# Linformer attention and maxout FFN on one core: batch 2's softmax sums moved into one bank, their broadcast issued from GpSimd, and later turns of q

## The chip, the cores and the metric

The kernel runs on one core of one Trainium2 chip. The metric is the device time of one execution in microseconds. Four runs of the kernel before gave a median of 403.85 us (403.59 to 404.13). The execution that was profiled took 402.95 us; its span, from the first to the last instruction of the program, was 401.2 us. The clock that was granted to TensorE was 0.999 of full speed over it.

## What is computed

Two stages follow each other. The first is attention with projected keys and values, for 8 batches of 8 heads, 1024 positions and 64 features a head; the second is a feed-forward layer with three parallel weights.

```python
k_proj = np.einsum('ks,bhsd->bhkd', E, k)          # E, F: 64 x 1024
v_proj = np.einsum('ks,bhsd->bhkd', F, v)
scores = scale * np.matmul(q, k_proj.transpose(0, 1, 3, 2))
attn = np.exp(scores - max) ; attn = attn / (sum + 1e-9)
x = attn @ v_proj          # then (b, s) rows of 8 * 64 = 512
h = np.maximum(np.maximum(x @ w1, x @ w2), x @ w3)   # 512 -> 768
out = h @ w_out                                      # 768 -> 512, float32
```

The kernel leaves the maximum out of the softmax, works in bf16 on TensorE and adds in float32.

## The kernel before, in words

**Tiling.** A batch has 1024 rows, cut into two chunks of 512. For a chunk, `up` (L609) makes one of six blocks of 128 hidden features: 12 matmuls (3 weights by 4 slices of the 512 inputs) into three PSUM banks. ScalarE copies the first bank to SBUF (`h1s`, L625), VectorE takes the maximum with the second (`m12`, L629) and then with the third, which gives a block of `hT` (L577). `down` (L655) makes four tiles of 128 output rows, 6 matmuls each; from batch 1 on ScalarE copies each tile to SBUF, and after every second tile SyncE issues the store of both (L678). So a chunk has ten steps: 0 to 5 are `up`, 6 to 9 are `down`. PSUM has eight banks; attention takes pairs of banks (`two`) or single ones (`bank`).

**Attention is done one batch ahead.** While the feed-forward matmuls of batch b run, the attention of batch b + 1 is put between them. `plan(b)` (L685) says behind which step of which chunk each piece is issued: key (chunk, step). All queues (TensorE, VectorE, ScalarE, GpSimd, SyncE) run in program order, so this dictionary is the order of work. The pieces:

- `load(b)` (L197): three DMAs on GpSimd's queue, q, k and v of a batch, cast to bf16 (1 MB each in SBUF). q has two buffers, k and v one each. So k's load waits for the projection of the batch before, and v's as well. The load of q of batch b waits until the turn of q of batch b - 1 has landed.
- `qd(b)` (L380): VectorE copies q into `q_p` in four instructions, then SyncE issues one DMA transpose of `q_p` into `qT`.
- `kproj`, `vproj` (32 matmuls at L345, copies on VectorE and ScalarE) and `kt` (2 transposes at L412): the projected keys and values.
- `sc(b, g)`: scores of a pair of heads, 4 matmuls of 64 x 64 (L211) that run side by side; I call four such matmuls a pack. ScalarE then takes the exponential (`pT`, L222): at once with `now=True`, or else queued in `later`, which is run behind the next copy that ScalarE makes for `up` or `down`.
- `za(b, g)`, the older form of the softmax sums: a pack with `ones` as weights (the sums, spread over the partitions), a pack with the projected values, then on ScalarE `invert` (a logarithm at L291 and an exponential at L297, each over 128 x 1024) which writes `zi_all`, then on VectorE the product `xT` (`scale_x`, L308).
- `zc(b)` (L248), the newer form: 8 matmuls with `pick` (L256) put the sums of all heads into one bank; ScalarE takes one logarithm (L262) and one exponential (L265) of 128 x 512; SyncE stores the 32 KB result to DRAM (`zd`, L268) and then issues four DMAs (L275) that broadcast it to 64 partitions each of `zi_all`, 512 KB a DMA; the first two are for head pairs 0 and 1, the last two for 2 and 3. `vx(b, g)` follows later: the values pack and the product `xT`.

In the kernel before, batches 1 and 2 use `za` (batch 0 has its own start), batches 3 to 7 use `zc` and `vx`. Batch 1's pieces are issued during batch 0, batch 2's during batch 1, and so on.

Of the kernel before, what the change touches and what calls it, by code (L numbers as in the profile page):

```python
# [15 lines left out]
def kernel(  # L16
# [13 lines left out]
    nc = tc.nc  # L30
# [77 lines left out]
    def after(dma, earlier):  # L108
        tc.add_manual_dep(
            dma.ins, earlier.ins.name,  # L110
            mybir.DependencyInfo(
                mybir.DependencyClass.Sync, mybir.DependencyReason.DATA
            ),
        )


    def view(src, b):
        return src[b].rearrange("h (p si) d -> p h si d", si=SI)
# [12 lines left out]
    qkv, qTs, kpTs, vps, pTs, zis, xTs = {}, {}, {}, {}, {}, {}, {}  # L131
# [5 lines left out]
    def load_tiles(b):  # L137
        qkv[b] = tuple(
            loads.tile([P, H, SI, D], BF16, name=nm, bufs=n)
            for nm, n in (("q_t", 2), ("k_t", 1), ("v_t", 1))  # L140
        )
        return qkv[b]
# [51 lines left out]
    load_w(2, slice(2, 4))  # L194
    nc.gpsimd.dma_start(out=wout_sb, in_=moe_w_out.rearrange("(jt p) m -> p jt m", p=P))

    def load(b):  # L197
        tiles = load_tiles(b)
        for i in range(3):
            dma = nc.gpsimd.dma_start(out=tiles[i], in_=view((q, k, v)[i], b))  # L200
            if i == 0 and b - 1 in last_T:
                after(dma, last_T[b - 1])
# [42 lines left out]
            zi_alls[b] = att.tile([P, NPAIR, 2, CHUNK], FP32, name="zi_all", bufs=1)  # L245
        return zi_alls[b]

    def zc(b):  # L248

        def f():
            t, ns = bank()
            for hp in range(2):
                for g in range(NPAIR):
                    nc.tensor.matmul(  # L256
                        out=t[32 * g:32 * (g + 1), :], lhsT=pick[:, hp, :],
                        rhs=pTs[b, g, 0][:, hp, :], start=(hp == 0), stop=(hp == 1),
                    )
            ready = pe(2 * MM + 0.1)  # L260
            zlc = att.tile([P, CHUNK], FP32, name="zlc", bufs=1)
            nc.scalar.activation(out=zlc, in_=t, func=AF.Ln)  # L262
            runs("s", ready, 0.6, ns)
            zic = att.tile([P, CHUNK], FP32, name="zic", bufs=1)
            nc.scalar.activation(out=zic, in_=zlc, func=AF.Exp, scale=-1.0)  # L265
            when = runs("s", ready, 0.63) + 9.0
            zd = scratch.tile([NPAIR, 2, 2, CHUNK], FP32, name="zd")
            nc.sync.dma_start(  # L268
                out=zd.rearrange("g h c f -> (g h c) f"),
                in_=zic.rearrange("(a r) f -> a r f", r=8)[:, 0, :],  # L270
            )
            for u in range(2):
                gs = slice(2 * u, 2 * u + 2)
                for hp in range(2):
                    nc.sync.dma_start(  # L275
                        out=zi_all(b)[hp * HALF:(hp + 1) * HALF, gs],
                        in_=zd[gs, hp].partition_broadcast(HALF),
                    )
            for g in range(NPAIR):
                zis[b, g, 0] = zi_all(b)[:, g], when  # L280
        return f

    def vx(b, g):
        def f():
            scale_x(b, g, 0, SI, values(b, g, 0, SI))
        return f
# [34 lines left out]
    def sc(b, g, lo=0, nsi=SI, now=False):  # L321
        def f():
            t = scores(b, g, lo, nsi)
            if now:
                exps(b, g, lo, nsi, t)
            else:
                later.append(lambda: exps(b, g, lo, nsi, t))
        return f

    def za(b, g, lo=0, nsi=SI, then=False):  # L330
        def f():
            z = sums(b, g, lo, nsi)
            av = values(b, g, lo, nsi)
            invert(b, g, lo, nsi, z)
            if then:
                later.append(lambda: scale_x(b, g, lo, nsi, av))
            else:
                scale_x(b, g, lo, nsi, av)
        return f
# [40 lines left out]
    def qd(b, parts=1):  # L380

        def f():
            q_p = att.tile([P, NPAIR, SI, 2, D], BF16, name="q_p", bufs=1)
            qTs[b] = att.tile([P, NPAIR * SI, P], BF16, name="qT")
            n = NPAIR // parts
            for lo in range(0, NPAIR, n):
                for g in range(lo, lo + n):
                    copy(
                        "v", q_p[:, g].rearrange("p si h d -> p h si d"),
                        qkv[b][0][:, 2 * g:2 * g + 2], (), 0.43,  # L390
                    )
                last_T[b] = nc.sync.dma_start_transpose(
                    out=qTs[b][:, lo * SI:(lo + n) * SI, :],
                    in_=q_p[:, lo:lo + n].rearrange("p g si h d -> p (g si h d)"),
                )
        return f

    kps = {}
    def kproj(b):
        def f():  # L400
            t, ns = bank()
            proj(b, 1, t, (LO, HI), 4 * D)
            kps[b] = att.tile([P, 2, 2 * D], BF16, name="kp")
            copy("v", kps[b].rearrange("a g x -> a (g x)"), t[:, 0:4 * D], ns, 0.43)
        return f

    def kt(b):
        def f():
            t, ns = two()
            t = t.bitcast(BF16)[:, 0]  # L410
            for gg in range(2):
                nc.tensor.transpose(  # L412
                    out=t[:, gg * P:(gg + 1) * P], in_=kps[b][:, gg, :], identity=ident
                )
            pe(0.2)

            kpTs[b] = att.tile([P, NPAIR, KP], BF16, name="kpT")
            copy(
                "v", kpTs[b].rearrange("a (y x) k -> a x y k", x=2),
                t[:, 0:2 * P].rearrange("a (x y k) -> a x y k", x=2, y=2), ns, 0.3,  # L420
            )
        return f

    def vproj(b):
        def f():
            t, ns = bank()
            proj(b, 2, t, (LO, HI), 4 * D)

            vps[b] = att.tile([P, H, D], BF16, name="vp")
            for hh, hs in enumerate((LO, HI)):  # L430
                i = t[hh * HALF:(hh + 1) * HALF, 0:4 * D].rearrange("a (h d) -> a h d", d=D)
                for to in range(2):
                    copy("sv"[hh], vps[b][to * HALF:(to + 1) * HALF, hs, :], i, ns, 0.4)
        return f
# [244 lines left out]

    def ld(b):
        return lambda: load(b)

    def plan(b):  # L685
        n = b + 1
        if b == 0:
            c1 = (SPC, SPC)
            return {
                (0, 6): [za(0, 1, *c1), sc(0, 3, *c1)],  # L690
                (0, 7): [qd(1, 2), za(0, 2, *c1)],
                (0, 8): [za(0, 3, *c1)],
                (1, 0): [kproj(1)],
                (1, 1): [kt(1)],
                (1, 2): [vproj(1), ld(2)],
                (1, (3, "mid")): [sc(1, 0), sc(1, 1)],
                (1, 4): [za(1, 0), sc(1, 2)],
                (1, 5): [za(1, 1), sc(1, 3)],
                (1, 7): [za(1, 2)],
                (1, 8): [za(1, 3)],  # L700
            }
        if b == 1:
            return {
                (0, 1): [qd(2)],
                (0, 5): [kproj(2), vproj(2), ld(3)],
                (0, 6): [kt(2)],
                (0, 7): [sc(2, 0)],
                (0, 9): [za(2, 0), sc(2, 1)],
                (1, 1): [za(2, 1), sc(2, 2)],
                (1, 3): [za(2, 2), sc(2, 3)],  # L710
                (1, 5): [za(2, 3)],
                (1, 6): [qd(3)],
            }
        if b == 2:
            return {
                (0, 0): [kproj(3), vproj(3), ld(4)],
                (0, 1): [kt(3)],
                (0, 2): [sc(3, 0, now=True), sc(3, 1)],
                (0, 4): [sc(3, 2, now=True), sc(3, 3)],
                (0, 6): [zc(3)],  # L720
                (0, 7): [qd(4)],
                (1, 3): [kproj(4), vproj(4), ld(5), vx(3, 0), vx(3, 1)],
                (1, 4): [kt(4)],
                (1, 6): [vx(3, 2), vx(3, 3), sc(4, 0)],
            }
        if n == B:
            return {}
        out = {
            (0, 1): [sc(n, 1, now=True), sc(n, 2, now=True), sc(n, 3)],
            (0, 3): [zc(n)],  # L730
            (1, 2): [vx(n, 0), vx(n, 1)],
            (1, 6): [vx(n, 2), vx(n, 3)],
        }
        if n + 1 < B:
            out[0, 2] = [qd(n + 1)]
            out[1, 2] = [kproj(n + 1), vproj(n + 1)] + out[1, 2]
            out[1, 3] = [kt(n + 1)]
            out[1, 6] += [sc(n + 1, 0)]
        if n + 2 < B:
            out[1, 3] += [ld(n + 2)]  # L740
        return out
# [61 lines left out]
```

The softmax here doesn't subtract the row's maximum and nothing guards it: scores larger than these inputs give would overflow.

## Time and profile before

| what | value |
|---|---|
| median of 4 runs | 403.85 us |
| the profiled execution, its own time | 402.95 us |
| its span | 401.2 us |
| TensorE busy | 392.8 us, 98% of the span |
| VectorE busy | 203.3 us, 51% |
| ScalarE busy | 156.0 us, 39% |
| the 1152 matmuls of `up` (L567) | 257.8 us busy |
| the 378 matmuls of `down` at L664 | 86.9 us busy |

The profile is that of one execution, a little shorter than the median. Busy times of matmuls overlap, since matmuls are pipelined: a 128 x 512 matmul lasts 379 ns in a row, but one starts every 216 ns. So the time that a group of matmuls takes of TensorE is read from the timeline, as the distance between the starts of what stands before and after it. In the timeline, a row has its start, its length, the engine, the line, what it writes and reads, how many instructions were merged, and in brackets the idle time before it and what ended that.

### The profile page before, as it was taken

Reading aid. Unit: us, or ns where it says so; the run is one execution under the profiler, and the core shown is the slowest. Engines: PE = TensorE matmul, PEld = TensorE weight load, DVE = VectorE, ACT = ScalarE, POOL = GpSimd, SP = SyncE. Lnnn points to the kernel's source line nnn. Section 1 sums busy time; section 2 is a strip of 40 time slices with the busy share of each in tenths; the row PEclk is TensorE's granted clock in tenths of the full one; section 3 lists DMA queues with packets and bytes.
Section 4 is the critical chain, followed back from the end, with each engine's and each line's share of the span. In section 5 each row is a group of like instructions: output and inputs, shape, how many; then the busy total and the mean of one; then the engine's idle time right before and its main releaser. Section 6 shows DMA issues by size and latency. Waiting matters only on the chain.

```text
span 401.2 us, 5795 instructions
## 1 busy us (share of the span) xinstructions
PE 392.8 (98%) x2311; PEld 176.8 (44%) x2311; DVE 203.3 (51%) x319; ACT 156.0 (39%) x244; POOL 31.4 (8%) x44
## 2 busy tenths in 40 slices
PE   7999999999999999999999999999999999999996
PEld 3544443344445445444444445444454444444443
DVE  2348755761755435735274634745166342745251
ACT  2622537525673542353313542245323533132322
POOL 7440001001000200200010000100000000000000
PEclk9999999999999999999999999999999999999999
DMA  9999999959908999999899689973850229020202
GB/s 151 206 206 207 231 209 162 244 119 166 245 11 209 153 172 238 194 226 199 152 251 247 172 165 250 235 194 72 185 167 2 105 64 252 3 106 0 105 2 105
DMA packets 65707, 63.98 MB, mean 159 GB/s; under 512 B 30528, under 2 KB 58688, under 8 KB 65680
## 3 DMA queue, kind: packets, MB, share of 16 engines
q0 software_dynamic: 28512, 28.31, 44.1%
q1 hardware_dynamic: 37024, 35.16, 33.0%
q8 instruction: 18, 0.29, 0.3%
q10 hardware_dynamic: 144, 0.13, 0.1%
q14 instruction: 9, 0.07, 0.1%
HBM read 67.63 MB, written 16.94 MB: 211 GB/s over the span
## 4 chain that ended last, share of the span: by engine, by line
PE 80%; DMA 12%; DVE 3%; ACT 3%; issue 1%; SPq 0%; DVEq 0%; ACTq 0%
PE banks L567 52%; PE banks L664 17%; DMA v_t<-in_v_dram 7%; PE banks L345 3%; PE banks L231 2%; DMA zi_all<-zd 2%; PE banks L211 2%; DVE xT L308 2%; DMA ef_f<-in_F_dram 1%; ACT zl L291 1%; ACT zi_all L297 1%; PE banks L441 1%; PE banks L256 1%; DVE hT L577 1%; DMA zd<-zic 1%
## 5 line engine op out<-in xcount | busy, mean ns | idle before, releaser
L567 PE MATMUL banks<-xT,w_sb 128*128 128x512 bf16 x1152 | 257.8, 379 | 0.4 <-DVE xT L308 0.2
L567 PEld LDWEIGHTS <-w_sb 128*128 128x128 bf16 x1152 | 109.8, 98 | 137.5 <-issue 10.1
L629 DVE TENSOR_TENSOR m<-banks,h1s 128x512 f32<-128x512 f32 x90 | 62.1, 690 | 125.9 <-ACT h1s L625 81.1
L625 ACT COPY h1s<-banks 128x512 f32<-128x512 f32 x90 | 52.7, 585 | 112.1 <-PE banks L567 109.9
L664 PE MATMUL banks<-wout_sb,hT 128*128 128x512 bf16 x378 | 86.9, 380 | 0.2
L577 DVE TENSOR_TENSOR hT<-banks,m 128x512 bf16<-128x512 f32 x90 | 62.3, 692 | 10.7 <-PE banks L567 1.7
L664 PEld LDWEIGHTS <-hT 128*128 128x128 bf16 x378 | 35.6, 98 | 47.4 <-issue 4.8
L102 ACT COPY o_sb<-banks 128x512 f32<-128x512 f32 (+1 forms) x56 | 32.6, 583 | 58.4 <-PE banks L664 58.2
L308 DVE TENSOR_TENSOR xT<-banks,zi_all 128x1024 bf16<-128x1024 f32 x28 | 33.4, 1221 | 22.5 <-ACT zi_all L297 13.3
L222 ACT ACTIVATE pT<-banks 128x1024 bf16<-128x1024 f32 (+1 forms) x36 | 32.8, 931 | 23.2 <-PE banks L211 23.2
L200 POOL DMA_DIRECT2D q_t<-in_q_dram x7 | 6.2, 880 | 190.1 <-DMA qT<-q_p 87.4
L291 ACT ACTIVATE zl<-banks 128x512 f32<-128x512 f32 (+1 forms) x16 | 13.0, 811 | 9.8 <-PE banks L231 8.9
L345 PEld LDWEIGHTS <-efT 128*64 128x64 bf16 x224 | 11.6, 110 | 3.6 <-issue 3.0
L102 DVE CAST vp<-banks 64x256 bf16<-64x256 f32 (+1 forms) x18 | 7.1, 397 | 11.1 <-ACT vp L102 8.0
L102 ACT CAST vp<-banks 64x256 bf16<-64x256 f32 x14 | 5.1, 366 | 19.2 <-PE banks L345 19.1
L231 PE MATMUL banks<-pT,vp 64*64 64x512 bf16 (+1 forms) x144 | 11.8, 362 | 0.4 <-DVE vp L102 0.4
L211 PE MATMUL banks<-qT,kpT 64*64 64x512 bf16 (+1 forms) x144 | 11.5, 361 | 0.0
L102 DVE COPY q_p<-q_t 128x1024 bf16<-128x1024 bf16 x28 | 10.0, 420 | 0.0
L297 ACT ACTIVATE zi_all<-zl 128x1024 f32<-128x1024 f32 x8 | 8.5, 1058 | 0.3
L102 DVE COPY o_sb<-banks 128x512 f32<-128x512 f32 (+1 forms) x9 | 5.8, 654 | 4.5 <-PE banks L644 4.5
L441 PE MATMUL banks<-warm_f 128*128 128x512 f32 x8 | 6.6, 977 | 1.5 <-DVE warm_f L175 1.5
L200 POOL DMA_DIRECT2D k_t<-in_k_dram x7 | 6.2, 879 | 19.7 <-PE banks L345 19.5
(59 smaller groups left out, 120.1 us busy)
## 6 DMA issues: line engine op xcount, KB each, us to landing
out_dram<-o_sb SPq DMA_DIRECT2D x30, 512.0 KB, 6.8
zi_all<-zd SPq DMA_DIRECT2D x20, 512.0 KB, 8.4
q_t<-in_q_dram POOLq DMA_DIRECT2D x7, 1024.0 KB, 13.4
k_t<-in_k_dram POOLq DMA_DIRECT2D x7, 1024.0 KB, 15.7
v_t<-in_v_dram POOLq DMA_DIRECT2D x7, 1024.0 KB, 19.9
w_sb<-in_moe_w_dram POOLq DMA_DIRECT2D x5, 384.0 KB, 12.0
k_t<-in_k_dram POOLq DMA_DIRECT2D x2, 512.0 KB, 9.0
v_t<-in_v_dram POOLq DMA_DIRECT2D x4, 256.0 KB, 12.2
```

Of the source, the lines that this page charges most:

```text
L102: done = {"v": nc.vector.tensor_copy, "s": nc.scalar.copy, "g": nc.gpsimd.tensor_copy}[eng](out=o, in_=i)
L211: nc.tensor.matmul(out=t[c * HALF:(c + 1) * HALF, hp, 0:n * P], lhsT=kpTs[b][rows, g, :], rhs=qTs[b][rows, at:at + n, :], start=True, stop ...
L222: nc.scalar.activation(out=pTs[b, g, lo], in_=t, func=AF.Exp, scale=scale)
L231: nc.tensor.matmul(out=t[hp * HALF:(hp + 1) * HALF, c, 0:nsi * HALF], lhsT=w(rows, hp), rhs=p[rows, hp, :], start=True, stop=True,)
L291: nc.scalar.activation(out=zl, in_=t, func=AF.Ln)
L308: nc.vector.tensor_tensor(out=xTs[b][:, g, lo:lo + nsi, :].rearrange("a (c s) p -> a c (s p)", c=2), in0=t, in1=zi, op=ALU.mult,)
L345: nc.tensor.matmul(out=t[hh * HALF:(hh + 1) * HALF, 0:width], lhsT=efT[:, si, (kv - 1) * KP:kv * KP], rhs=qkv[b][kv][:, heads[hh], si, :], ...
L567: nc.tensor.matmul(out=h, lhsT=w_sb[i][:, ct, jt * P:(jt + 1) * P], rhs=xTs[b][:, ct, ch * SPC:(ch + 1) * SPC, :], start=(ct == first), st ...
L577: nc.vector.tensor_tensor(out=o, in0=h, in1=other, op=ALU.max)
L625: nc.scalar.copy(out=h1s, in_=h[0][0])
L629: nc.vector.tensor_tensor(out=m12, in0=h[1][0], in1=h1s, op=ALU.max)
L664: nc.tensor.matmul(out=o_ps, lhsT=hTs[b, ch][:, jt, tt * P:(tt + 1) * P], rhs=wout_sb[:, jt, :], start=(jt == 0), stop=(jt == NJT - 1),)
```

## The change

Three things are changed. In batch 1's plan, batch 2's attention gets the newer form: `zc(2)` and four `vx(2, g)` in place of four `za(2, g)`. The four broadcasts of `zc(2)` are issued on GpSimd's queue and not on SyncE's; the store of `zd` stays on SyncE. The load of batch 3 is split: q and k are issued behind the projections of batch 2, v behind those broadcasts on the same queue. The pieces of batch 2's attention are placed one or two steps earlier, and `qd(3)` too, from (1, 6) to (1, 1). In batch 2's plan all pieces of the first chunk stand one step later. In the plans of batches 3, 4 and 5 the turn of q, `qd(n + 1)`, goes from (0, 2) to (0, 4), so that on SyncE its transpose stands behind the broadcasts of `zc(n)` at (0, 3).

```diff
-    def load(b):
-        tiles = load_tiles(b)
-        for i in range(3):
+    def load(b, which):
+        tiles = qkv[b] if b in qkv else load_tiles(b)
+        for i in which:
             dma = nc.gpsimd.dma_start(out=tiles[i], in_=view((q, k, v)[i], b))
...
-    def zc(b):
+    def zc(b, queue=nc.sync):
...
-                    nc.sync.dma_start(
+                    queue.dma_start(
                         out=zi_all(b)[hp * HALF:(hp + 1) * HALF, gs],
                         in_=zd[gs, hp].partition_broadcast(HALF),
                     )
...
         if b == 1:
             return {
-                (0, 1): [qd(2)],
-                (0, 5): [kproj(2), vproj(2), ld(3)],
-                (0, 6): [kt(2)],
-                (0, 7): [sc(2, 0)],
-                (0, 9): [za(2, 0), sc(2, 1)],
-                (1, 1): [za(2, 1), sc(2, 2)],
-                (1, 3): [za(2, 2), sc(2, 3)],
-                (1, 5): [za(2, 3)],
-                (1, 6): [qd(3)],
+                (0, 0): [qd(2)],
+                (0, 3): [kproj(2), vproj(2), ld(3, (0, 1))],
+                (0, 4): [kt(2)],
+                (0, 5): [sc(2, 0, now=True), sc(2, 1, now=True), sc(2, 2)],
+                (0, 6): [sc(2, 3)],
+                (0, 8): [zc(2, nc.gpsimd), ld(3, (2,))],
+                (1, 1): [qd(3)],
+                (1, 3): [vx(2, 0), vx(2, 1)],
+                (1, 6): [vx(2, 2), vx(2, 3)],
             }
         if b == 2:
             return {
-                (0, 0): [kproj(3), vproj(3), ld(4)],
-                (0, 1): [kt(3)],
-                (0, 2): [sc(3, 0, now=True), sc(3, 1)],
-                (0, 4): [sc(3, 2, now=True), sc(3, 3)],
-                (0, 6): [zc(3)],
-                (0, 7): [qd(4)],
+                (0, 1): [kproj(3), vproj(3), ld(4)],
+                (0, 2): [kt(3)],
+                (0, 3): [sc(3, 0, now=True), sc(3, 1)],
+                (0, 5): [sc(3, 2, now=True), sc(3, 3)],
+                (0, 7): [zc(3)],
+                (0, 8): [qd(4)],
                 (1, 3): [kproj(4), vproj(4), ld(5), vx(3, 0), vx(3, 1)],
                 (1, 4): [kt(4)],
                 (1, 6): [vx(3, 2), vx(3, 3), sc(4, 0)],
...
         if n + 1 < B:
-            out[0, 2] = [qd(n + 1)]
+            out[0, 4] = [qd(n + 1)]
             out[1, 2] = [kproj(n + 1), vproj(n + 1)] + out[1, 2]
```

More of the change, by code (lines that the diff above doesn't have):

```diff
@@ L678, in down, with ld @@
             nc.sync.dma_start(out=ov[:, si - 1:si + 1, :], in_=o_sb)
-    def ld(b):
-        return lambda: load(b)
+    def ld(b, which=(0, 1, 2)):
+        return lambda: load(b, which)
     def plan(b):
```

## The prediction

> **What bounds the kernel now.** I read the engine table first, then the shares of the chain that ended last, then TensorE's timeline for its gaps, then the queues.
>
> ```profile
> PE 392.8 (98%) x2311; PEld 176.8 (44%) x2311; DVE 203.3 (51%) x319; ACT 156.0 (39%) x244; POOL 31.4 (8%) x44
> PE 80%; DMA 12%; DVE 3%; ACT 3%; issue 1%; SPq 0%; DVEq 0%; ACTq 0%
> ```
>
> TensorE is busy 98% of the span and is 80% of the chain. So only two things can move the time: what TensorE itself runs, and the few places where it stands. The timeline of TensorE shows the first of these places, ScalarE's timeline the reason.
>
> ```profile
> 93.12 1.46 PE L664 MATMUL banks<-wout_sb,hT 128*128 128x512 bf16 x6
> 94.51 0.41 PE L211 MATMUL banks<-qT,kpT 64*64 64x512 bf16 x4
> 94.85 2.76 PE L664 MATMUL banks<-wout_sb,hT 128*128 128x512 bf16 x12
> 97.92 0.41 PE L231 MATMUL banks<-pT,ones 64*64 64x512 bf16 x4 [0.30 <-ACT pT L222]
> ...
> 98.69 0.61 PE L567 MATMUL banks<-xT,w_sb 128*128 128x512 bf16 x2
> ```
> ```profile
> 96.36 0.59 ACT L102 COPY o_sb<-banks 128x512 f32<-128x512 f32 x1 [1.16 <-PE banks L664]
> 96.84 1.03 ACT L222 ACTIVATE pT<-banks 128x1024 bf16<-128x1024 f32 x1
> ```
>
> The scores of 94.51 get their exponential only behind the copy of the tile that follows them: copy 1.51 us after that tile's first matmul, exponential .48 later, 1.03 long, .05 more until TensorE goes on: 3.07 us. TensorE needs 2.59 us for two tiles (12 x .216) and .11 to change to packs, so it stands 3.07 - 2.70 = .37 us. This pattern returns below.
>
> The second place is in batch 3; the chain and SyncE's queue show it.
>
> ```profile
> 193.05 2.14 DMA zd<-zic
> ...
> 195.86 9.85 DMA zi_all<-zd
> ...
> 205.84 1.24 DVE xT L308
> ...
> 207.12 0.27 PE banks L412 x2
> ```
> ```profile
> 182.20 10.76 SPq L392 DMA_TRANSPOSE qT<-q_p  x1
> 193.05 0.55 SPq L268 DMA_DIRECT2D zd<-zic  x1
> 195.21 2.78 SPq L275 DMA_DIRECT2D zi_all<-zd  x4
> ```
>
> SyncE issues the transpose of q(5) for 10.76 us, since loads of batch 5 fill the DMA engines; the sums, ready on ScalarE at 184.38, are stored only at 193.05. The broadcast lands at 205.72, the products run late, and `kt` waits for their banks: the matmuls from 203.66 (x12) should end at 206.25, `kt` starts at 207.12. That is .85 us.
>
> **Batch 2's attention (in batch 1).** Prices of groups, from the distances in TensorE's timeline less .216 for each feed-forward matmul: one pack .44 (94.41 to 94.85), two .66 (115.99 to 116.65), three .88 (103.87 to 104.75), the 8 `pick` matmuls .65 (142.08 to 142.73). Before: .44 + (.88 + .37 wait) + .88 + .88 + .66 = 4.11. After: three score packs .88, one .44, `zc` .65, two groups of values .66 each = 3.29. So **-.82**, of which .37 is the wait. But `sc(2, 3)` has its exponential behind the copy of tile (0, 7), and `zc(2)`, which needs it, comes two tiles later: the pattern above, **+.37**.
>
> ScalarE also loses four pairs of 1.03 and 1.06 us and gains .60 and .63; it is 39% busy, so this is worth nothing. `qd(2)`, one step earlier, puts 1.4 us of copies behind VectorE's work of step 0; q(2) landed at 68.55 and five banks are free, so nothing. Its transpose passes the DMA queue 1.6 us earlier, at 80.1, and lands near 87; so q(3) loads from 87.4 (before 88.90) and k(3) behind it. `kproj(2)` at 84.7 needs v(2), landed at 80.65: 4 us of cover. `kt` keeps its price.
>
> **The new wait: the broadcast on GpSimd.** Batch 1 starts at 73.87 in both. Scores come at 91.9, `zc(2)` at 97.1, and at 97.5 with its wait. Its result is on ScalarE 1.93 later (182.45 to 184.38 in batch 3): 99.4. `zd` goes on SyncE behind the store of two tiles issued at 96.5, while k(3) is loading. The `zd` at 144.13, beside a load, took 4.56; that store's like (95.23) took 7.0. Both give about 104.0; without load 2.1 gives 101.5. GpSimd's issues start .55 after what they wait for (88.35 to 88.90): 104.5. Two broadcasts land 7.25 after the first issue where nothing runs beside (327.14 to 334.39), 10.5 beside a load (195.21 to 205.72). I take 7.25, since k(3) is through by about 103 and v(3) is queued behind; plus .23, for GpSimd issues take .88 where SyncE's take .65; plus .5 for the transpose of q(3), which SyncE issues from 106.8. In the trace's packets the queues take turns packet by packet: 135 of a transpose (256 B) went beside 150 of a load (1 KB) in a microsecond, so small packets take little from 4 KB ones. That makes 112.5.
>
> Needed by: `vx(2, 0)` and `vx(2, 1)` end at 110.4. Behind the waiting product on VectorE stand the other product, then the maxima of steps 4 and 5, and tile 0's last matmul waits for those. In batch 4 the row from the first product's start (252.47) to the end of that chain (about 257.6 without `kt`'s copy) is 5.14 us. The last matmul's natural time is 116.62, so the product may start at 111.4 at the latest. **+1.1**, bounds 0 (109.3 by the fastest rows) to 3.9 (115.3 by the slowest). The second pair lands near 119 and may until 120.5. v(3), issued behind the broadcasts near 108, lands near 123 and is needed at 128 plus the delay: this is where moving the first chunk of batch 2 by a step gives it cover.
>
> The Trainium skill (DMA: Bandwidth & Descriptors, Issuing engines are not separate DMA queues) says that DMAs issued from different engines share the same 16 engines and that only issue time is saved; it speaks against any gain from the other queue, and the packets taking turns agree. Its Specifications there put the first byte at about 1 us for GpSimd's path and 0.6 for SyncE's; as an estimate from that page the sum would be .4 higher.
>
> **Batch 2's plan, a step later.** `sc(3, 3)` now has its exponential behind tile (0, 6)'s copy, with `zc(3)` two tiles on; before, it lay behind a step's copy with time to spare (no wait at 142.18). **+.37**. `zc(3)` moves by 1.3 us. Its broadcast landed at 156.16 (first pair) for products at 160.73: cover 4 us. `qd(4)` stays behind it on SyncE; qT(4) landed at 166.32 for scores at 166.91, only .6 of cover, but now a store less stands between: I cost it at nothing, and at .5 if not. q(4)'s load waits for qT(3), then k(4) and v(4) for the projections 2.6 later: needed 30 us on, nothing.
>
> **Turns of q in batches 3 to 5.** `zd` of batch 4 goes at 184.4 instead of 193.05, its broadcast lands near 197 and is needed at 204.8: **-.85**. What is late next is nothing: qT(5) lands near 206 for scores at 214.5, the load of q(6) starts then (before 195.56), k(6) is needed at 248. The stores behind the transpose on SyncE wait, with three buffers of output. VectorE's four copies now stand before step 5's maxima: 180.71 to 182.05 is 1.34; from 186.41 they end at 187.75 where the maximum started at 187.60; its block is ready at 189.23, needed at 189.21. About .02 three times, **+.06**.
>
> **Sum.** -.82 + .37 + 1.1 + .37 - .85 + .06 = +.23. On the profiled execution's 402.95 that is 403.2; its span is 1.75 less than that, outside the change. The median lies .9 above it: 403.85 + .23 = **404.1 us**. This kernel can hardly be told from no change within 0.2%, .81 us.
>
> **Rivals.**
> - The broadcast is in time (`zd` lands at 102.5 or sooner, or the pair in under 7): the sum is -.87, **403.0**. For it: k(3) starts 1.5 us earlier. Against: the store ahead of `zd` in SyncE's queue. Chance .20.
> - Slower: GpSimd's broadcasts share the DMA engines with SyncE's store and the transpose of q(3), and the first pair takes 9 to 10.5 us as at 195.21. The product starts at 114 to 115.3, the sum is +1.7 to +3.0, about **406**. It decides from a landing at 113.1 on. For it: the one row with a neighbour. Against: that neighbour was a 1 KB load, this one has 256 B packets. Chance .25.
> - The change doesn't do what it says in batch 3, because the earlier broadcast meets the loads of batch 5, or qT(4) is late: +.85 or +.5 more, **404.9**. Against: it has 16 us. Chance .10.
> - The forecast, .45; its own range 403.2 to 404.6.
>
> **Range.** 402.9 to 405.8: both ends of the broadcast's bounds but the last fifth. Faster .20, same .45, slower .35.
>
> **What would show it.** TensorE idle before `zc(2)` and `zc(3)` on pT, about .3 in the brackets, and no idle before the sums of batch 2; VectorE idle before the first product of batch 2 on `zi_all`, and tile 0 of batch 1's second chunk waiting for `hT`; in batch 3 no wait before L412, `zd` at 184.4. I am wrong if the broadcast lands before 111 or after 113, or if `zc` does not wait.

## The result and the profile after

The changed kernel takes 402.74 us in the median of 41 runs (402.0 to 404.77), the kernel before 403.88 in 66 runs made with them. The ratio is 0.9975, interval [0.9967, 0.9982]: it is faster by about 1.0 us. That lies below the range of the prediction (402.9 to 405.8), by .16 at its lower end.

One thing must be set apart before the profiles can be compared. The profiled execution of after took 403.01 us, that of before 402.95, and both spans are 401.2 us, as if nothing had changed. The chain of waits of after, in its first part, shows why: it goes through the first weights.

```profile
6.34 13.62 DMA w_sb<-in_moe_w_dram
```

Batch 1 starts at 74.97 instead of 73.87. Over all thirteen profiles of this study the first matmul of batch 1 stands anywhere between 73.87 and 76.18; two profiles of the unchanged kernel have 73.87 and 75.16. The two latest, 76.03 and 76.18 (`pool_fill`, `sync_bcast`), are those in which the granted clock was .5 for 3.4 us ahead of batch 1; such an execution has .996 or less in the mean. So the start is no part of the change, and from here on a batch's length is the distance between the first `up` matmuls of it and of the next (of the last batch, to the start of its last matmul).

| kernel | batch 1 | 2 | 3 | 4 | 5 | 6 | 7 | sum |
|---|---|---|---|---|---|---|---|---|
| before | 47.97 | 49.28 | 47.57 | 46.49 | 46.72 | 44.29 | 41.35 | 323.67 |
| after | 47.89 | 49.63 | 46.52 | 46.52 | 46.52 | 44.29 | 41.35 | 322.72 |
| difference | -.08 | +.35 | -1.05 | +.03 | -.20 | 0 | 0 | -.95 |

The sum, -.95, is near the measured -1.0; that it comes so near is in part luck, since batch 1 of after and batch 3 of before turn out below to differ by .9 between executions. The gain is in batches 3 and 5, in whose plans only the turn of q was moved; batches 1 and 2, where the new sums are, lose .27 together. The engine table and the shares of the chain change little:

```profile
PE 392.1 (98%) x2303; PEld 176.6 (44%) x2303; DVE 202.9 (51%) x319; ACT 149.2 (37%) x238; POOL 34.1 (9%) x48
...
PE 82%; DMA 11%; DVE 3%; ACT 2%; POOL 1%; issue 1%; DVEq 0%; ACTq 0%; POOLq 0%
```

TensorE has 8 matmuls fewer (16 of the old sums go, 8 of `pick` come), ScalarE 6 instructions and 6.8 us less, GpSimd four more DMA issues. In TensorE's timeline of after, the group of packs with the .30 wait is gone, and the wait stands two tiles later:

```profile
95.53 2.76 PE L664 MATMUL banks<-wout_sb,hT 128*128 128x512 bf16 x12
98.22 0.97 PE L256 MATMUL banks<-pT,pick 128*32 128x512 bf16 x8
99.12 1.25 PE L664 MATMUL banks<-wout_sb,hT 128*128 128x512 bf16 x5
...
111.44 5.35 PE L567 MATMUL banks<-xT,w_sb 128*128 128x512 bf16 x24
116.63 1.24 PE L664 MATMUL banks<-wout_sb,hT 128*128 128x512 bf16 x5
118.09 0.39 PE L664 MATMUL banks<-wout_sb,hT 128*128 128x512 bf16 x1 [0.22 <-DVE hT L577]
```
```profile
97.03 0.59 ACT L102 COPY o_sb<-banks 128x512 f32<-128x512 f32 x1 [0.21 <-PE banks L664]
97.52 1.03 ACT L222 ACTIVATE pT<-banks 128x1024 bf16<-128x1024 f32 x1
```

The row at 98.22 is `zc(2)`: eight matmuls that take .62 elsewhere take .97, with no bracket, because the wait fell inside the group: its first three matmuls use scores of which the exponential is done, the fourth waits for that of `sc(2, 3)`, which ScalarE (second fence) starts at 97.52 behind a copy and ends at 98.55. In after the brackets alone would not show this .35; the length of the row does. The last row of the first fence is the other new wait: tile 0 of the second chunk, for hT. `zc(3)` shows the same .97:

```profile
144.50 0.97 PE L256 MATMUL banks<-pT,pick 128*32 128x512 bf16 x8
```

In batch 3, SyncE's queue has `zd` and the broadcasts ahead of the transpose, and the wait before L412 is gone:

```profile
185.78 0.53 SPq L268 DMA_DIRECT2D zd<-zic  x1
190.91 2.54 SPq L275 DMA_DIRECT2D zi_all<-zd  x4
193.56 10.65 SPq L392 DMA_TRANSPOSE qT<-q_p  x1
```
```profile
205.06 2.76 PE L567 MATMUL banks<-xT,w_sb 128*128 128x512 bf16 x12
207.66 0.28 PE L412 MATMUL banks<-ident,kp 128*128 128x128 bf16 x2
```

### The profile page after: what moved, and what is told of

It reads as the page before. It is cut to its first block, busy times and chain, and to the rows that moved or that the text cites. A ratio compares the mean times of both kernels' runs of the same rounds, so it can differ in the third digit from the quotient of the medians.

```text
span 401.2 us, 5779 instructions
## 1 busy us (share of the span) xinstructions
PE 392.1 (98%) x2303; PEld 176.6 (44%) x2303; DVE 202.9 (51%) x319; ACT 149.2 (37%) x238; POOL 34.1 (9%) x48
## 4 chain that ended last, share of the span: by engine, by line
PE 82%; DMA 11%; DVE 3%; ACT 2%; POOL 1%; issue 1%; DVEq 0%; ACTq 0%; POOLq 0%
PE banks L567 55%; PE banks L664 18%; DMA v_t<-in_v_dram 7%; DMA w_sb<-in_moe_w_dram 3%; PE banks L345 3%; PE banks L231 2%; PE banks L211 2%; DVE xT L308 1%; PE banks L256 1%; ACT zi_all L297 1%; ACT zl L291 1%; DVE m L629 0%; DVE hT L577 0%; POOL k_t L152 0%; POOL v_t L152 0%
## 5 line engine op out<-in xcount | busy, mean ns | idle before, releaser
L291 ACT ACTIVATE zl<-banks 128x512 f32<-128x512 f32 (+1 forms) x12 | 8.9, 740 | 5.2 <-PE banks L231 4.4
L345 PE MATMUL banks<-v_t,efT 128*64 128x256 bf16 x112 | 7.3, 273 | 0.3 <-DMA v_t<-in_v_dram 0.3
L345 PE MATMUL banks<-k_t,efT 128*64 128x256 bf16 x112 | 7.5, 276 | 0.0
```

Source lines behind the costliest of these rows:

```text
L291: nc.scalar.activation(out=zl, in_=t, func=AF.Ln)
L345: nc.tensor.matmul(out=t[hh * HALF:(hh + 1) * HALF, 0:width], lhsT=efT[:, si, (kv - 1) * KP:kv * KP], rhs=qkv[b][kv][:, heads[hh], si, :], ...
```

## The experiments

My theory after this comparison: the two parts of the change add up, the turn of q brings what batches 3 and 5 gained, the new sums cost the .27 of batches 1 and 2. The rival: batch 3's wait hangs on something else that both parts move, so that either alone removes it. Eleven kernels were run; each ratio is to the kernel before on the same chip.

**Each part alone.** `turn_only`, the kernel before with

```diff
-            out[0, 2] = [qd(n + 1)]
+            out[0, 4] = [qd(n + 1)]
```

> The kernel before with one edit: qd(n + 1) in the plans of batches 3 to 5 at (0, 4) and not (0, 2). My theory, after the two traces: the gain of the whole change is made here. Batch 3 gets shorter from 47.57 to about 46.5 us (no wait of .85 before L412, since zd goes when it is ready), batches 4 and 5 change by less than .1, unless the wait of .22 us for the last block of hT in batches 3 and 5 moves as well. Sum -.85 to -1.3 us, batches 1 and 2 stay at 47.97 and 49.28. The rival, that batch 2's new sums make the gain and the turn is worth little, expects less than .3 us here.

Measured: 402.45 us, ratio 0.9973 [0.9961, 0.9985]. Batches 1 and 2 are those of before (47.96, 49.27); batch 3 is 46.75, batch 5 is 46.75. `zd` is issued at 184.59, and the wait of .85 has gone, as forecast. But batches 3 and 5 are each .23 longer than in after, so the turn alone doesn't explain batch 5's gain at all.

`form_only`, the kernel after with that one line put back to `out[0, 2]`:

> The changed kernel with qd(n + 1) back at (0, 2): so only batch 2's new sums and what goes with them. My theory: batch 1 about 47.9 us (before 47.97), batch 2 about 49.6 (before 49.28), batch 3 stays at about 47.5 with its wait before L412; in all +.2 to +.3 us against the kernel before, less .2 to .4 if the waits of .22 us for hT move. The rival expects -.8 us or more here, the worth of the packs that fall away.

Measured: 403.08 us, ratio 0.9978 [0.9969, 0.9987]: also faster, by .9 us. Batch 1 is 48.82 (the wait for hT is 1.12 here, .38 in after, and the block before it stands .20), batch 2 is 49.63, and batch 3 is 46.49 without the moved turn. So the rival holds: `zd` and the broadcasts are as late as in before, and still nothing waits before L412. The plan of batch 1 is the same in `form_only` and in after, so the .93 by which batch 1 differs is a difference between executions:

```profile
118.39 0.39 PE L664 MATMUL banks<-wout_sb,hT 128*128 128x512 bf16 x1 [0.95 <-DVE hT L577]
```

SyncE's queue, GpSimd's and TensorE's timeline of `form_only` in batch 3:

```profile
183.87 9.70 SPq L392 DMA_TRANSPOSE qT<-q_p  x1
193.66 0.54 SPq L268 DMA_DIRECT2D zd<-zic  x1
196.51 2.68 SPq L275 DMA_DIRECT2D zi_all<-zd  x4
```
```profile
197.23 0.88 POOL L200 DMA_DIRECT2D q_t<-in_q_dram  x1 [26.62 <-DMA qT<-q_p]
```
```profile
207.93 0.28 PE L412 MATMUL banks<-ident,kp 128*128 128x128 bf16 x2
```

Yet the pair lands 8.25 us after its first issue, and 10.5 in before. What differs is GpSimd's issue of q(6)'s load, which waits for qT(5): in before at 195.56, .35 us after the first broadcast; here .72 after. In before's packets from 198 to 201 us the load moves up to 128 packets of 1 KB per us, and those of the second broadcast (4 KB) fall to 6 per us; in `form_only` the broadcasts have 46 to 61 per us from 198 to 202, and the load's first packet comes at 201.3. So 114 of the pair's 256 packets have gone in before when the load's first one starts, and 180 in `form_only`.

**Is that race the cause?** `pool_fill` is the kernel before with six small instructions more on GpSimd, ahead of batch 3's load, which do nothing that the output uses. They only move GpSimd's later instructions by six places.

```diff
+    fill = const.tile([P, 1], FP32, name="fill")
...
+        [nc.gpsimd.memset(fill, 0.0) for _ in range(6 * (b == 3))]
```

> The kernel before, with six memsets of one element a partition on GpSimd ahead of the load of q(3), at a time when GpSimd is idle. They cost nothing by themselves. In the run with batch 2's form alone, the wait of .85 us before L412 in batch 3 was gone although zd still stood behind the transpose of q(5); there GpSimd issued the load of q(6) .91 us after what it waits for, and in the kernel before .56, in time to get its packets between the first and the second broadcast. The number of GpSimd's instructions ahead of it is larger by six there. My theory: the six memsets shift the pause of GpSimd's queue to the same place, q(6)'s load is issued .9 us after qT(5) has landed, the first pair takes about 8 us instead of 10.5, and batch 3 gets shorter from 47.57 to 46.7: -.85 us for six instructions that do nothing. If batch 3 stays at 47.4 or more with a load that came later, the race at the start isn't the cause; if the load still comes .56 us after, the pause does not go by the count of instructions, and the run says nothing on the race.

Measured: 402.51 us, ratio 0.9947 [0.992, 0.9974]. Batch 3 is 46.72. GpSimd now issues the load .91 after qT(5) has landed instead of .56, so .71 after the first broadcast (issued at 197.23) instead of .35; the pair lands 7.26 after its first issue (242 of its 256 packets have gone when the load's first one starts), and the wait is gone:

```profile
197.94 0.88 POOL L200 DMA_DIRECT2D q_t<-in_q_dram  x1 [26.15 <-DMA qT<-q_p]
```
```profile
208.41 0.28 PE L412 MATMUL banks<-ident,kp 128*128 128x128 bf16 x2
```

The wait that the turn of q was to remove is a race between two queues, which .36 us of issue time decides. Six empty instructions win it as well as the moved turn does (batch 3 is 46.72, and 46.75 in `turn_only`).

**How fixed is the wait?** `before_again` is the kernel before, unchanged, profiled a second time.

> The kernel before, unchanged, profiled again: is the wait of .85 us in batch 3 there each time? My theory says yes: batches 1 to 7 last what they lasted before, within .05 us, with 47.57 for batch 3, and q(6)'s load comes .56 us behind qT(5). Only the time ahead of batch 1 differs, by what the first loads take. If batch 3 comes out near 46.7, the wait is chance, and the comparison of single profiles proves less than I take from it.

Measured: 403.75 us, ratio 0.9998 [0.9978, 1.0018]. All batches repeat within .01, except batch 3: 48.48 instead of 47.57. (The x11 is a group of twelve of which the trace has lost one record.)

```profile
205.16 2.54 PE L567 MATMUL banks<-xT,w_sb 128*128 128x512 bf16 x11 [0.16 <-issue]
209.29 0.27 PE L412 MATMUL banks<-ident,kp 128*128 128x128 bf16 x2 [1.59 <-DVE xT L308]
```
```profile
208.01 2.36 DVE L308 TENSOR_TENSOR xT<-banks,zi_all 128x1024 bf16<-128x1024 f32 x2 [1.89 <-DMA zi_all<-zd]
```

Its load was issued .37 after the first broadcast and the first product began 11.54 after it (10.63 in the first profile). So the wait was there both times, with .85 and 1.76 us: a gain counted against one profile is uncertain by .9. This can also account for ratios that lie below what a trace shows against the first profile (`form_only` -.11 by its batches against -.9 measured). `pool_fill`'s ratio, -2.1 us with an interval that reaches -1.05, is still more than the -.85 and -1.75 that its batches give against the two. The clock can account for the rest: of the 31 runs of the kernel before on its chip 11 had a mean granted clock of .996 or less, of its own 11 runs one; the medians of the others are 402.50 and 403.83, a gain of 1.3. The ratios of `turn3_late`, `sync_bcast` and `sync_held` below are taken to the same 31 runs.

**Batch 5, and .23 more in batch 3.** In before, VectorE paused before the last hT block of these two batches for about .4 us though its input was there, and TensorE stood .23 for it (batch 5 is 46.72, and 46.49 in `form_only`). In batch 5 of before:

```profile
306.17 0.69 DVE L577 TENSOR_TENSOR hT<-banks,m 128x512 bf16<-128x512 f32 x1 [0.46 <-PE banks L567]
```

Counted from 0 along VectorE's records in the trace, waits for semaphores included, the two late hT blocks are numbers 319 and 447, 128 apart (none is late at 255 and 383). After has two records fewer (557, not 559), so these blocks are numbers 317 and 445, and 319 and 447 are first products, which stand idle 1.56 us for their banks anyway. The next place in the same step is number 191: in before it is a first maximum, which stands about .4 in every batch, but in after it is an hT block, and it is .41 late. `two_more_after` puts two back at the start, the kernel after with

```diff
-    nc.vector.memset(ones, 1.0)
+    for _ in range(3):
+        nc.vector.memset(ones, 1.0)
```

> The changed kernel with two more memsets of a 128 x 64 tile on VectorE in the first microseconds, where VectorE is idle. They cost nothing by themselves. In the kernel before, the last block of hT started about .4 us late in batches 3 and 5 for no reason that the waits show; these were the instructions 319 and 447 of VectorE's queue in the trace, and 63, 191, 319 and 447 lie 128 apart. In the changed kernel the same instructions are the numbers 317 and 445 and are not late. If a pause of VectorE's queue at every 128th (or 64th) instruction is the cause, two more instructions put it back: batches 3 and 5 get longer by .2 us each, from 46.52 to about 46.74, +.4 us in all. If the pause belongs to something else (banks, the DMA queues, the plan), nothing changes.

Measured: 403.15 us, ratio 0.9988 [0.9975, 1.0001]. Batches 3 and 5 are 46.75 and 46.76: +.23 and +.24, for two small instructions that stand in the preparation, over 190 us earlier. VectorE's timeline in batch 5, first of `two_more_after`, then of after (the bracket is idle time; its releaser, TensorE, had long been done):

```profile
305.07 0.69 DVE L629 TENSOR_TENSOR m<-banks,h1s 128x512 f32<-128x512 f32 x1 [0.73 <-PE banks L567]
306.21 0.69 DVE L577 TENSOR_TENSOR hT<-banks,m 128x512 bf16<-128x512 f32 x1 [0.45 <-PE banks L567]
```
```profile
305.39 0.69 DVE L629 TENSOR_TENSOR m<-banks,h1s 128x512 f32<-128x512 f32 x1 [0.73 <-PE banks L567]
306.19 0.69 DVE L577 TENSOR_TENSOR hT<-banks,m 128x512 bf16<-128x512 f32 x1
```

From the start of the maximum to that of hT it is 1.14 us with the pause and .80 without. So -.46 of the change's -.95, .23 in each of the two batches, comes from where VectorE's instructions fall in its count. Batch 1 of `two_more_after` is 48.10, with a wait for hT of .59. Why pauses stand 128 apart is not settled. The Trainium skill (Runtime: NRT & Kernel Launch, Instruction fetch mechanics) says that an engine's instructions are fetched in blocks of 16 KiB, 256 instructions, and calls the cost of crossing a block mostly hidden. A fixed step along the count would fit a fetch, but no run shows that it is one, and the step here is 128 records; and .23 on TensorE's path was not hidden here.

**Where v(3) and the broadcasts stand.** Two kernels issue batch 2's broadcasts on SyncE. `sync_bcast` is after with

```diff
-                (0, 8): [zc(2, nc.gpsimd), ld(3, (2,))],
+                (0, 8): [zc(2), ld(3, (2,))],
```

> The changed kernel with the four broadcasts of zc(2) on SyncE's queue instead of GpSimd's; the load of v(3) is written at the same place, but nothing holds it back now, and it follows k(3) at once. My theory: what GpSimd's queue is worth is the order, v(3) behind the broadcasts. Here v(3)'s load fills the DMA engines while the broadcasts start, and the first pair of them takes 9 to 10 us from its first issue (in the changed kernel 7.2); the first product of batch 2 is 1.5 to 2.5 us later, batch 1 gets longer from 47.9 to 49.4 to 50.4 us. The rival, that only the issuing engine's speed matters, expects SyncE's earlier start (.5 us) to take the wait of .4 us for hT away: batch 1 about 47.5.

Measured: 405.64 us, ratio 1.0029 [1.0007, 1.0051]. Nothing holds v(3) now; GpSimd issues it at 91.33 and it runs beside the broadcast, of which the pair takes 9.5 us (106.73 to 116.25). Batch 1 is 50.16, +2.27 on after:

```profile
117.65 1.89 PE L567 MATMUL banks<-xT,w_sb 128*128 128x512 bf16 x7 [1.38 <-DVE xT L308]
121.57 0.39 PE L664 MATMUL banks<-wout_sb,hT 128*128 128x512 bf16 x1 [0.96 <-DVE hT L577]
```

`sync_held` is `sync_bcast` with v(3)'s load made to wait for batch 2's last broadcast:

```diff
+                    last_zi[b] = queue.dma_start(
...
+            if (b, i) == (3, 2):
+                after(dma, last_zi[2])
```

> As sync_bcast, but the load of v(3) waits until the last broadcast has landed. Both theories expect the broadcasts to start .5 us earlier than on GpSimd, ahead of the store that SyncE issues next, and the first pair to take about 7.3 us: the wait of .4 us (.4 to 1.1 in the runs so far) for hT in batch 1 goes, batch 1 about 47.5 us. If batch 1 stays at 47.9 or more, the sum for the broadcast's landing is wrong in another term. v(3) then lands near 125, with 3 us to spare.

Measured: 409.66 us, ratio 1.011 [1.0074, 1.0146]. Its first half came as expected: the pair lands 7.7 us after its first issue (104.05 to 111.75), hT's wait is down to .19, batch 1 is 47.69. The second half failed. I had given v(3) 3 us to spare; issued at 116.63 it took 16.6 us, as long as in after (16.66, issued at 108.20), and batch 2 is 57.33:

```profile
133.27 1.92 PE L347 MATMUL banks<-v_t,efT 128*64 128x256 bf16 x16 [5.09 <-DMA v_t<-in_v_dram]
```

This wait of 5.09 is not the whole loss of 7.70 on after: from 131.5 to 138.4 us the granted clock was .50 (the 16 matmuls of this row take 1.92, those of k(3) before the wait 1.06), and half speed over the 5.1 us from 133.27 on costs about 2.5 (an estimate). The loss differs between executions; the ten runs go from 404.77 to 410.38.

So the engine that issues the broadcasts is worth little in itself: the pair takes 7.2 to 7.6 on GpSimd and 7.7 on SyncE, and lands 37.59 after batch 1's start with SyncE, 37.80 to 38.73 with GpSimd. What counts is the order that one queue gives: v(3)'s load issued after the broadcasts are issued, but not held until they have landed.

**Is the transpose of q(3) what makes the broadcast late?** `turn3_late` moves `qd(3)` in after:

```diff
-                (1, 1): [qd(3)],
...
-                (1, 6): [vx(2, 2), vx(2, 3)],
+                (1, 6): [vx(2, 2), vx(2, 3), qd(3)],
```

> The changed kernel with qd(3) back at (1, 6) of batch 1, behind vx(2, 2) and vx(2, 3): so no DMA transpose runs beside the broadcasts of zc(2). In the prediction I put the transpose's share at .5 us. If that was right, the first pair lands 6.7 us after its first issue and not 7.2 to 7.6, and v(3) much earlier. If small packets take nothing from large ones, the pair still takes 7.2 to 7.6, and only SyncE's own time for the transpose falls from 17.4 us to about 5 to 10. VectorE's four copies go behind the last products, which may make batch 2 start .1 to .3 us later.

Measured: 403.04 us, ratio 0.9968 [0.9943, 0.9992]. The pair takes 7.32 us, and 7.17 in after. But this does not price a transpose beside a broadcast, for there is none in after: SyncE issues it at 107.92, its first packet of 256 B moves at 114.35, and the pair has landed at 112.77. So the transpose costs this pair nothing because it comes too late to meet it. The wait for hT is .75, not smaller: counted from batch 1's start `zd` lands .22 later here than in after and the pair .36 later.

**The waits of `zc`.** `now` gives the exponential of `sc(2, 3)` and `sc(3, 3)` its place ahead of the tile's copy on ScalarE:

```diff
-                (0, 6): [sc(2, 3)],
+                (0, 6): [sc(2, 3, now=True)],
...
-                (0, 5): [sc(3, 2, now=True), sc(3, 3)],
+                (0, 5): [sc(3, 2, now=True), sc(3, 3, now=True)],
```

> The changed kernel, with the exponentials of sc(2, 3) and sc(3, 3) issued at once (now=True) and not behind the copy of the next tile. If the waits of .36 us inside the pick matmuls of zc(2) and zc(3) come from that order on ScalarE, as I worked out before the result, both go: the copy of the tile then stands behind the exponential, .5 us later, and has a bank's time to spare. Batch 1 from 47.89 to about 47.5, batch 2 from 49.63 to about 49.27, in all -.7 us against the changed kernel. The rival, that ScalarE only shifts the wait (the copy of the tile comes late and the next tile waits for a bank), expects less than .2 us.

Measured: 403.06 us, ratio 0.9986 [0.9965, 1.0007]; by its batches -.37 on after. Both waits are gone; `zc(2)` is a row of

```profile
97.62 0.62 PE L256 MATMUL banks<-pT,pick 128*32 128x512 bf16 x8
```

and batch 2 is 49.27, .36 shorter. The 12 runs, 401.82 to 405.4, are too spread to show this gain on after. Batch 1 stays at 47.89: TensorE comes .36 earlier to tile 0, the broadcast does not, and the wait for hT grows from .38 to .73. One wait was covering the other.

**Versions made from this.** `now_split` is `now` with the second products put behind the maxima that tile 0 needs:

```diff
-                (1, 3): [vx(2, 0), vx(2, 1)],
-                (1, 6): [vx(2, 2), vx(2, 3)],
+                (1, 3): [vx(2, 0)],
+                (1, 6): [vx(2, 1), vx(2, 2), vx(2, 3)],
```

> The changed kernel with the exponentials at once (as in the run named now) and vx(2, 1) moved from (1, 3) to (1, 6). In now, the wait inside zc(2) went, but tile 0 of the second chunk waited for hT .35 us longer, since the broadcast did not come any earlier: batch 1 stayed at 47.89. With one product and not two between the broadcast and the maxima of steps 4 and 5, the chain on VectorE is 1.2 us shorter, so the first product may start 1.2 us later. I expect no wait for hT in batch 1: 47.1 to 47.3 us, batch 2 at 49.27, batches 3 to 5 at 46.52, in all -2.0 us against the kernel before and about -1 against the changed one. If the wait for hT only moves to the first matmuls of batch 2 (three products behind tile 0), batch 1 or 2 keeps .3 us or more of it.

Measured: 401.7 us, ratio 0.995 [0.9932, 0.9967]. Batch 1 is 47.19, .70 shorter than in `now`. VectorE still waits 1.77 us for the broadcast, but only one product stands ahead of the maxima, and tile 0 waits for nothing:

```profile
112.02 1.23 DVE L308 TENSOR_TENSOR xT<-banks,zi_all 128x1024 bf16<-128x1024 f32 x1 [1.77 <-DMA zi_all<-zd]
```
```profile
114.98 1.50 PE L664 MATMUL banks<-wout_sb,hT 128*128 128x512 bf16 x5
116.41 0.84 PE L231 MATMUL banks<-pT,vp 64*64 64x512 bf16 x12
```

`turn_now30` leaves the new sums out: the kernel before with the moved turn, the exponential of `sc(2, 0)` put first, and 30 small instructions on VectorE at the start, which move its pauses elsewhere.

```diff
-                (0, 7): [sc(2, 0)],
+                (0, 7): [sc(2, 0, now=True)],
...
     nc.vector.memset(ones, 1.0)
+    [nc.vector.memset(ones[:, 0:1], 1.0) for _ in range(30)]
...
-            out[0, 2] = [qd(n + 1)]
+            out[0, 4] = [qd(n + 1)]
```

> The kernel before with three small edits and without batch 2's new sums: qd(n + 1) at (0, 4); the exponential of sc(2, 0) at once; 30 memsets of one element a partition on VectorE at the start, which shift the pause at every 128th instruction of VectorE's queue from the last hT block of a chunk to an instruction that waits 7 us anyhow. By the theory: batch 1 from 47.97 to 47.6 (no wait for pT), batch 2 49.27, batches 3 to 5 46.5 each (in turn_only 46.75, 46.52, 46.75): -1.6 us against the kernel before, more than the change as a whole, which says that the change's own part, the new sums, is worth about nothing as it stands. If the pause doesn't follow the count, batches 3 and 5 stay at 46.75.

Measured: 401.74 us, ratio 0.9946 [0.9929, 0.9962]. Batches 3 and 5 are 46.52 each, without the pauses; batch 1 is 47.58, -.39 for the one wait. Both versions are faster than before by about 2 us; against after, whose ratio is 0.9975, that is about 1. From batch 1 on they sum to 321.67 (`now_split`) and 322.06: by these two profiles the new sums, when their waits are removed, are worth .39; as changed, they cost .27. The times, 401.70 and 401.74, don't tell the two apart.

## Why the prediction was wrong

The forecast was +.23; the batches show -.95.

| step of the prediction | forecast | in the profiles |
|---|---|---|
| packs of batch 2 in batch 1 | -.82 | -.82 (what is left of batch 1's -.08) |
| `zc(2)` waits for its exponential | +.37 | +.36 |
| the new wait: the broadcast on GpSimd | +1.1 | +.38; .59 and 1.3 in two more profiles |
| `zc(3)` waits likewise in batch 2 | +.37 | +.35 |
| turns of q, the wait before L412 | -.85 | -.85, or -1.76 against the second profile |
| VectorE's copies, three batches | +.06 | +.09 (.03 each, after against `form_only`) |
| VectorE's pauses in batches 3 and 5 | none | -.46 |

The forecasts add up to +.23, the first numbers on the right to -.95.

- **The step that failed is "the new wait: the broadcast on GpSimd", +1.1, by its size.** In after it is +.38. The mechanism was right: VectorE waits for `zi_all` (1.21 us), and tile 0's last matmul for hT. Up to the landing of `zd` the sum was exact: counted from batch 1's start, 30.08 instead of 30.13. The pair was priced too long. I added .23, since GpSimd issues loads every .88 us, and .5 for the transpose beside it: 7.98. It was 7.17:

```profile
105.60 2.61 POOL L275 DMA_DIRECT2D zi_all<-zd  x4 [15.41 <-DMA zd<-zic]
108.20 0.92 POOL L200 DMA_DIRECT2D v_t<-in_v_dram  x1
```

GpSimd issues four broadcasts in 2.61, .65 each, as SyncE does; it is the load that takes .9. The transpose moved no packet before the pair had landed. So the row without a neighbour, 7.25, was near the price (7.17 to 7.61 in the six kernels that issue these broadcasts on GpSimd), and neither addition had a ground. The limit held: landing at 112.77, in before's clock 111.7, the wait was .38.

But .38 is one execution. In the profiles with the same plan of batch 1, after, `two_more_after` and `form_only`, batch 1 is 47.89, 48.10 and 48.82, where the prediction's steps make 48.62; in the last, `zd` lands at 30.58, the pair takes 7.61, and the waits sum to 1.3. So this step accounts for -.72 of the -1.18 between forecast and batches in the profile shown, and for less or nothing in others.

- **A term put at nothing: VectorE's pauses, -.46.** With the -.72 they make the -1.18 in the profile shown. This part of the miss does not vary: the pauses are in both profiles of before and not in after. No step had them. Before's trace held the wait, an hT block that starts .4 after its input is there, and I didn't ask what ended it; I looked only for waits that the change was meant for. That its end depends on the count of instructions could not be read from one profile.
- **The turn of q** has its -.85 against the profile shown, but for a reason that I had only half: the late `zd` alone does no harm (`form_only`, `pool_fill`); late together with an early load of q(6), it does. The new sums move that load as well, so the two parts do not add, and the loss varies (.85 and 1.76). How much of it stands in the median of before's 66 runs, two profiles can't say.
- **The range** took its lower end from the broadcast's bound alone; it treated the -.85 as exact, and left no room for what the unpriced waits of before might do.
- What else was to show did show: `zc(2)` and `zc(3)` waiting (in the rows' lengths, not in brackets), no wait before batch 2's sums, `zd` of batch 4 at 185.78, which is 13.29 us after batch 3's start (forecast 184.4, 13.28 after it). The rival with a neighbour, 9 to 10.5 us, came true only where v(3) was let loose (`sync_bcast`, 9.5).

## What to carry to other kernels

Before a wait is counted as a gain, look at it in a second profile of the same kernel, and ask which two things race there: .36 us of issue time decided about .85 to 1.76 us here, and it went with the edit that was meant for it (`turn_only`), with the other part of the change (`form_only`) and with six empty instructions (`pool_fill`). Test the parts of a change apart, for one part can take credit for what any shift would have brought. Where an engine starts late on an input that has long been there, count its instructions before blaming the data, and put work that the next matmul needs ahead of work that waits for a DMA.

## What the runs showed of the hardware

- VectorE pauses .40 us at places 128 apart in its records in the trace (seen at hT blocks 319 and 447 of before, 191 of after), and adding or removing two small instructions moves .23 us per batch on or off TensorE's path.
- A load that starts crowds out a running broadcast: in the second microsecond after its first packet the load has 115 and 106 packets of 1 KB in the two profiles of before, 93 in `form_only`, 117 in `pool_fill`, and the broadcasts have 1, 0, 28 and 41 of 4 KB. Some microseconds later both go on at about 50 each, in all four. What .36 us of issue time changes is how much of the pair has gone when the load's first packet moves: 114 and 115 of 256 packets in before, 180 and 242 in the other two. The Trainium skill (DMA: Bandwidth & Descriptors, Queues, rings and completion order) has each engine go round the queues packet by packet; if the trace's packets are the page's, the later stretch agrees with that, and the start of the load, a hundred packets to one in before, does not.
- A load beside a pair of broadcasts costs it 2.3 us (9.5 in `sync_bcast`, 7.17 in after). v(3)'s load, 1 MB, takes 16.66 us from its issue in after and 16.60 in `sync_held`, with a transpose under way each time, and 15.26 in `turn3_late` without it. Why so long, was not found.
- In `sync_held` TensorE waits from 128.2 to 133.27, and its granted clock is .50 from 131.5 to 138.4 us. No other profile here has .50 between the start of batch 1 and the last matmul.
